# Repacking attention outputs before normalizing them, two blocks at a time

## The chip, the cores and the metric

The kernel runs on one core of a Trainium2 chip. The metric is the time of one execution on the device, in microseconds (us); lower is better. The kernel before was timed three times: 1481.99, 1484.75 and 1485.82 us, median 1484.75. One further execution was profiled.

The core has five engines that run beside each other: PE (TensorE, matrix products), ACT (ScalarE, functions such as the exponential), DVE (VectorE), POOL (GpSimd) and SP (SyncE, which here only issues DMAs). Matrix products are written to PSUM, which has eight banks; everything else lies in SBUF.

## The reference, cut to what matters

Two equal layers, each an attention part A and a part B, with one set of weights for both:

```
x = x + A(layernorm(x))
x = x + B(layernorm(x))
x = x + A(layernorm(x))
x = x + B(layernorm(x))

A: q = (x @ wq) as 32 heads of 16;  k = x @ wk;  v = x @ wv    (one k and v for all heads)
   p = softmax(q k^T * 16**-0.5);  o = p v;  return o @ wo
B: h = gelu(layernorm(x) @ w1); each quarter of h is shifted by 1, -1, 2 or -2 rows; hs = h @ w2
   x1 = x + hs;  return x1 + gelu(layernorm(x1) @ w3) @ w4
```

x has 2048 rows (128-row tiles 0 to 15) of 512 columns in bfloat16. The softmax is over 2048 keys, for 32 heads and 2048 queries. Its denominator can be divided out after the product with v, and that division is what the change is about.

## The kernel before, in words

**Chunks, blocks, halves.** The queries of a layer are worked on in chunks of 512 rows (the last 512 of layer 1 as two chunks of 256). A chunk has eight blocks of four heads. A block goes over 16 key tiles of 128 keys; one key tile (two of them in a 256-row chunk) gives two halves of two heads each. There are 2048 halves in the program.

**Two ways for a half.** As a unit (`declare_unit`): PE makes the scores in two PSUM banks, ACT takes the exponential of 128x1024 scores at once (L1125), PE multiplies it with v (L1230). As a pair (`declare_pair`): PE makes the scores of each head in one of three shared banks, DVE turns each into the bits of an approximate exponential (L1143, two per half), POOL, or DVE when POOL is behind, makes two shifted copies (L1180), and PE multiplies all three with scaled copies of v (L1230). The shares on ACT and on DVE follow from the rules below. A column of ones in v gives the denominator as an extra row.

**The end of a block** (`block_end`). The sums lie in bank ACC: four strips of 32 partitions, of which the first 16 are the outputs of one head for half of the queries and row 16 is the denominator. DVE copies them to ACCF (L1264; blocks that had been put aside between the layers are added from there, L1260). PE gathers the denominators as columns (L1274), DVE takes reciprocals into RZ (L1281), PE spreads each over 32 partitions by a product with the identity (L1289), and DVE multiplies ACCF with that into OS (L1295). Then eight DMAs from SP repack OS into OT (L1318), where the output projection (`outproj`, L676 with L1450) wants 16 rows per head. For the last three blocks of a layer's last chunk (`LATE_OT` = 5) PE repacks with a selection matrix (L1308) and DVE copies the result to OT (L1314). When all eight blocks of a chunk are done, `chunk_end` declares the output projection, part B and, at the end of layer 0, the next layer's normalization, keys and values (`next_kv`: `ln_in`, `kv`, with the keys written at L943). This is called side work.

**Between the layers.** While the side work of layer 0's last chunk runs, layer 1 starts with the keys that are there: seven blocks (`SPILLED`) over key tiles 0 to 5 and then 6 to 10 (`EARLY`), their sums put aside (L1248, L1242) and added later.

**What sets the order.** Before anything is emitted, a planner simulates the engines with a duration for each operation and picks, engine by engine, the ready operation with the lowest priority number. The result is one fixed list of instructions per engine, with semaphore waits. Exponentials and their scores come first, then products with v, then pairs and side work. `assign` decides when a pair is started: `MAX_PAIRS` in flight, a limit on DVE's waiting side work (`BACKLOG`), two free shared banks. These and other rules change every 12.5 us of planned time, by one character of the string `TEMPER`, which picks a row of `MOODS`; characters 7, e and f are rows with three pairs in flight. Between the layers (layer 1, first chunk, key tiles below 11) the pair rule is `CALM`, whatever the row says: at most one pair in flight, backlog at most 1. Where PE would be idle too long the planner inserts filler products (L676, ONES and NIL)[...].[...]

Of the kernel before, what the change touches and what calls it, by code (L numbers as in the profile page):

```python
# [10 lines left out]
ALU = mybir.AluOpType  # L11
# [498 lines left out]
def t_ps(n):  # L510
    return 0.066 + n * 1.043e-3
# [6 lines left out]
def t_x2(n):  # L518
    return 0.066 + n * 0.522e-3
# [6 lines left out]
def tiled(n, k=1):  # L526
    return ("P", n * k, n * k, range(4))
# [6 lines left out]
class Kernel:  # L534
# [19 lines left out]
    CALM = (1, 1)  # L554
    CALM_END = (2, 1)
    LATE_OT = 5
# [33 lines left out]
    TEMPER = "090ee27f7f97f71e3eee4ee77f547c4fe941e77e7385715f85317197105502005897e0e10e0ef77f27f593f70f1f030e1e77ee0975325855000003"  # L590
# [9 lines left out]
    def sb(self, name, shape, dtype=dt.bfloat16):  # L600
        n = 1
        for s in shape:
            n *= s
        ap = self.stack.enter_context(self.nc.sbuf_tensor(name, [128, n], dtype))[:, :]
        self.sbytes += n * dt.size(dtype)
        return self.shaped(ap, shape)
# [9 lines left out]
    def memory(self):  # L616
        self.sbytes = 0
        sb = self.sb
# [19 lines left out]
        self.OS = sb("OS", [1024])  # L638
# [13 lines left out]
        self.RZ = sb("RZ", [32])  # L652
# [14 lines left out]
        p = self.par(1, 1)  # L667
# [42 lines left out]
    def head(self):  # L710
        pl = self.pl
        op = pl.op
        ins = self.ins
# [14 lines left out]
        def fill(eng, ap, v, tags, dur, prio):  # L728
            op(eng, lambda e: e.memset(ap, v), writes=tags, dur=dur, prio=prio)
# [38 lines left out]
        fill("POOL", self.SELC, 0.0, [("SELC",)], 0.1, 3)  # L768
        op("POOL", lambda e: e.affine_select(out=self.SELC, in_=self.SELC, compare_op=ALU.not_equal,
# [249 lines left out]
    def make_groups(self):  # L1019
# [49 lines left out]
        self.fin_left = {}  # L1069
        self.main_done = False  # L1070
# [167 lines left out]
    def block_end(self, la, c, b, end):  # L1238
# [13 lines left out]
        nq = n // 128  # L1252
        m = self.nfin % (1024 // n)
        self.nfin += 1
        parts = range(2 * m, 2 * m + 2) if n == 512 else (m,)
        am, zm, om = ([(x, i) for i in parts] for x in ("ACCF", "RZ", "OS"))
        acc, rz, osm = self.ACCF[:, m * n:m * n + n], self.RZ[:, 4 * nq * m:4 * nq * (m + 1)], self.OS[:, m * n:m * n + n]
# [8 lines left out]
        fin = min(5, self.RUSH[la][c])  # L1266
        L = Late()
# [11 lines left out]
        def frec(e):  # L1279
            with self.nc.allow_low_precision("the reciprocals feed a bf16 matmul"):  # L1280
                return e.reciprocal(rz, self.PB[:, L.bank, 0:4 * nq])  # L1281
        op("DVE", frec, writes=[L] + zm, dur=0.17, prio=fin, give=L)
        M = Late()
        for h in range(nq // 2):
            def fx(e, h=h):
                ins = None
                for q in (2 * h, 2 * h + 1):
                    for g in range(4):
                        ins = e.matmul(self.PB[32 * g:32 * g + 32, M.bank, q * 128:(q + 1) * 128],  # L1289
                                       lhsT=rz[:, 4 * q + g:4 * q + g + 1].to_broadcast([128, 32]),  # L1290
                                       rhs=self.IDENT, start=True, stop=True, tile_position=(0, 32 * g))
                return ins
            op("PE", fx, reads=zm + [("ID",)], writes=[M], pe=("P", 256, 256, range(4)), prio=fin,
               take=M if h == 0 else None)
        op("DVE", lambda e: e.tensor_tensor(out=osm, in0=acc, in1=self.PB[:, M.bank, 0:n],  # L1295
                                            op=ALU.mult),
           reads=am, writes=[M] + om, dur=t_ps(n), prio=fin, give=M)
        r0 = 64 * (b % 2)
        hw = n // 2
        if c == len(self.CHUNKS[la]) - 1 and b >= self.LATE_OT:  # L1300
            N = Late()

            def fo(e):
                ins = None
                for u in range(2):
                    for p in range(2):
                        x = r0 + 32 * p
                        ins = e.matmul(self.PB[x:x + 32, N.bank, u * hw:u * hw + hw], lhsT=self.SELO[:, u, :],  # L1308
                                       rhs=osm[:, p * hw:p * hw + hw], start=True, stop=True,
                                       tile_position=(0, x), skip_group_check=True)  # L1310
                return ins
            op("PE", fo, reads=om + [("SELO", i, u) for i in range(2) for u in range(2)], writes=[N],
               pe=("P", 2 * hw, hw, (r0 // 32, r0 // 32 + 1)), prio=fin, take=N)
            op("DVE", lambda e: e.tensor_copy(self.OT[r0:r0 + 64, b // 2, 0:n], self.PB[r0:r0 + 64, N.bank, 0:n]),  # L1314
               writes=[N, ("OT", b)], dur=t_ps(n), prio=fin, give=N)
        else:
            op("SP", lambda e: [
                e.dma_start(self.OT[r0 + 16 * (2 * p + i):r0 + 16 * (2 * p + i) + 16, b // 2, u * hw:u * hw + hw],  # L1318
                            osm[32 * (2 * i + u):32 * (2 * i + u) + 16, p * hw:p * hw + hw])
                for p in range(2) for i in range(2) for u in range(2)],  # L1320
               reads=om, writes=[("OT", b)], dma=128 * n, parts=8, prio=fin)
# [6 lines left out]
        if not left:  # L1328
            self.chunk_end(la, c)

# [309 lines left out]
```

## Time and profile before

| | |
|---|---|
| median of three runs | 1484.75 us (1481.99 to 1485.82) |
| the profiled execution's own time | 1481.02 us |
| its span in the profile | 1479.2 us |
| PE busy | 1454.1 us |
| ACT busy | 1421.3 us |
| DVE busy | 1285.0 us |
| POOL busy | 1146.2 us |
| exponentials on ACT (L1125) | 1419 |
| evictions of pairs on DVE (L1143) | 1258 |
| TensorE clock granted | 0.999 of full speed |

A line of the groups names the source line, engine and operation, what is written and from what, the shapes (partitions x elements), the count, then the busy time in us and the mean of one in ns, then the idle time of the engine just before them and what ended it. The mean of one can be longer than busy time divided by count, since neighbours overlap. Busy PE is not PE at its peak. In a table of windows a row has the window's start, end and length, then for each engine busy time and count in brackets (PE, weight loads, DVE, ACT, POOL), then the clock, the DMA share and GB/s.

### The profile page before, as it was taken

What the parts mean: (1) busy time and instruction counts of PE and PEld (TensorE: products, weight loads), DVE (VectorE), ACT (ScalarE), POOL (GpSimd) and SP (SyncE); (2) the same over time, 40 slices, a digit from 0 to 9 for tenths busy, and PEclk for the clock granted to TensorE, in tenths of its full rate; (3) what the DMA queues carried; (4) which work ended last, traced back from release to release, by engine and by line L of the source; (5) the groups of instructions that cost most, each with busy time, mean ns of one, the idle gap of its engine ahead of it and who ended that gap; (6) DMA issues with size and microseconds to landing.
All of it is one profiled execution on the core that took longest, in us unless ns stands there. A gap on an engine that the chain in (4) does not pass through costs nothing.

```text
span 1479.2 us, 66152 instructions
## 1 busy us (share of the span) xinstructions
PE 1454.1 (98%) x30189; PEld 651.1 (44%) x30189; DVE 1285.0 (87%) x2304; ACT 1421.3 (96%) x1511; POOL 1146.2 (77%) x817
## 2 busy tenths in 40 slices
PE   9999999999999999999999999999999999999999
PEld 4443434444444444444344444444444445555555
DVE  8989999989999979887886799999889989888863
ACT  7999999999999999999999999999999999999962
POOL 2788888878889878797765588889678898888640
PEclk9999999999999999999999999999999999999999
DMA  6100100001000000100000000010000000000000
GB/s 216 29 6 6 21 6 6 5 6 20 7 4 6 6 4 7 20 5 2 3 2 3 3 8 12 5 21 5 10 18 8 4 6 7 13 19 11 6 14 25
DMA packets 32153, 21.71 MB, mean 15 GB/s; under 512 B 12672, under 2 KB 31360, under 8 KB 31872
## 3 DMA queue, kind: packets, MB, share of 16 engines
q1 hardware_dynamic: 31872, 17.47, 5.0%
q8 instruction: 236, 3.87, 1.1%
q14 instruction: 45, 0.37, 0.1%
HBM read 7.90 MB, written 2.10 MB: 7 GB/s over the span
## 4 chain that ended last, share of the span: by engine, by line
ACT 74%; PE 21%; DVE 3%; POOL 1%; issue 0%; DMA 0%; POOLq 0%
ACT EA L1125 69%; PE PB L676 7%; PE PB L1081 7%; PE PB L1230 6%; ACT G L1573 3%; ACT L1125 1%; DVE J L1143 1%; ACT GP L1493 1%; POOL J L1180 1%; ACT L1573 1%; ACT L1493 1%; PE PB L875 1%; DVE ST L791 0%; DVE G L1568 0%; PE PB L932 0%
## 5 line engine op out<-in xcount | busy, mean ns | idle before, releaser
L1125 ACT ACTIVATE EA<-PB 128x1024 bf16<-128x1024 f32 x1419 | 1305.2, 1169 | 11.3 <-PE PB L1081 5.3
L1180 POOL TENSOR_SCALAR J<-J 128x2048 uint16<-128x2048 uint16 (+1 forms) x556 | 1006.1, 1810 | 233.5 <-DVE J L1143 126.4
L1143 DVE TENSOR_SCALAR J<-PB 128x512 uint16<-128x512 f32 x1258 | 808.5, 682 | 84.3 <-PE PB L1081 79.0
L1081 PE MATMUL PB<-QT,KT 32*128 32x512 bf16 (+1 forms) x4608 | 606.0, 360 | 13.7 <-ACT EA L1125 5.7
L1230 PE MATMUL PB<-J,VD 128*32 128x256 bf16 (+1 forms) x8448 | 413.9, 265 | 2.1 <-POOL J L1180 0.8
L1230 PE MATMUL PB<-EA,VP 128*32 128x256 bf16 (+1 forms) x6400 | 350.8, 263 | 0.7 <-DVE KT L1242 0.4
L1081 PEld LDWEIGHTS PB<-QT,KT 32*128 32x128 bf16 x4608 | 162.7, 91 | 385.0 <-ACT EA L1125 316.6
L1230 PEld LDWEIGHTS PB<-J,VD 128*32 128x32 bf16 x8448 | 176.1, 95 | 176.0 <-issue 133.9
L1230 PEld LDWEIGHTS PB<-EA,VP 128*32 128x32 bf16 x6400 | 150.3, 95 | 114.0 <-issue 90.9
L676 PE MATMUL PB<-ZT,W 128*32 128x512 bf16 (+2 forms) x2816 | 171.1, 342 | 0.2
L676 PE MATMUL PB<-W,G 128*32 128x512 bf16 x1624 | 104.2, 381 | 0.6 <-ACT G L1573 0.6
L1180 DVE TENSOR_SCALAR J<-J 128x2048 uint16<-128x2048 uint16 (+1 forms) x107 | 78.9, 737 | 8.8 <-POOL J L1180 7.9
L1568 DVE CAST G<-PB 128x512 bf16<-128x512 f32 (+2 forms) x126 | 72.5, 582 | 13.5 <-PE PB L676 12.2
L676 PEld LDWEIGHTS PB<-ZT,W 128*32 128x32 bf16 x2816 | 63.6, 96 | 33.5 <-issue 21.3
L811 POOL TENSOR_TENSOR SM<-SM,MH 128x2 f32<-128x2 f32 (+1 forms) x69 | 49.6, 722 | 22.2 <-DVE SM L813 13.5
L1573 ACT ACTIVATE G<-G 128x1792 bf16<-128x1792 bf16 x29 | 47.0, 1685 | 15.4 <-DVE G L1568 15.3
L676 PEld LDWEIGHTS PB<-W,G 128*32 128x32 bf16 x1624 | 37.5, 96 | 39.1 <-issue 11.6
L1295 DVE TENSOR_TENSOR OS<-ACCF,PB 128x512 bf16<-128x512 bf16 (+1 forms) x72 | 44.7, 621 | 7.3 <-PE PB L1289 7.0
L676 PE MATMUL PB<-ONES,NIL 128*32 128x512 bf16 x532 | 49.1, 400 | 1.6 <-DVE J L1143 0.5
L791 DVE BATCH_NORM_STATS2 ST<-X 128x6 f32<-128x512 bf16 x64 | 43.1, 681 | 1.8 <-DMA X<-in_A_x_dram 1.3
L1549 POOL TENSOR_TENSOR X<-Y,X 128x512 bf16<-128x512 bf16 x32 | 38.6, 1218 | 6.3 <-DVE Y L1531 4.6
L1264 DVE CAST ACCF<-PB 128x512 bf16<-128x512 f32 (+1 forms) x65 | 40.0, 615 | 2.5 <-PE PB L1230 2.4
(103 smaller groups left out, 765.7 us busy)
## 6 DMA issues: line engine op xcount, KB each, us to landing
OT<-OS SPq DMA_DIRECT2D x424, 8.0 KB, 1.8
W<-in_B_w_dram SPq DMA_DIRECT2D x2, 1792.0 KB, 14.9
X<-in_A_x_dram SPq DMA_DIRECT2D x8, 256.0 KB, 4.7
QT<-QS SPq DMA_DIRECT2D x32, 64.0 KB, 2.4
out_dram<-OUTB SPq DMA_DIRECT2D x16, 128.0 KB, 1.7
OT<-OS SPq DMA_DIRECT2D x104, 4.0 KB, 2.2
W<-in_B_w_dram SPq DMA_DIRECT2D x2, 512.0 KB, 9.3
WQ<-in_A_wq_dram SPq DMA_DIRECT2D x1, 512.0 KB, 4.1
```

Source lines behind the costliest of these rows:

```text
L676: ins = e.matmul(self.PB[32 * g:32 * g + 32, bank, 0:n], lhsT=lhsT[:, 32 * g:32 * g + 32], rhs=rhs, start=start, stop=stop, tile_position= ...
L791: op("DVE", lambda e, tb=tb: e.bn_stats(self.ST6[:, tb, :], src(tb)), reads=[tagf(tb)], writes=[("ST", tb)], dur=0.606, prio=prio)
L811: op("POOL", lambda e: e.tensor_tensor(out=out, in0=src, in1=self.MH[:, 0, a:b], op=ALU.pow), reads=tags + [("MH",)], writes=tg(r), dur=0. ...
L1081: ins = e.matmul(self.PB[:, bank, j * n:(j + 1) * n], lhsT=self.KT[32 * h:32 * h + 32, la, (kb + j) * 128:(kb + j + 1) * 128], rhs=self.QT ...
L1125: o = q.feeds = op("ACT", lambda e: e.activation(self.EA[:, ea, :, :], self.PB[:, b0:b0 + 2, :], ACTF.Exp, scale=0.25), writes=bk + [("EA" ...
L1143: o = op("DVE", lambda e, i=i, L=L: e.tensor_scalar(out=self.J[:, 3 * s, i * 512:(i + 1) * 512], in0=self.PB[:, L.bank, :], scalar1=128 * ...
L1180: o = self.pl.op(eng, lambda e: e.tensor_scalar(out=self.J[:, d, :], in0=self.J[:, f, :], scalar1=float(self.STEP), scalar2=1.0, op0=ALU.a ...
L1230: ins = e.matmul(self.PB[32 * x:32 * x + 32, self.ACC, p * hw:p * hw + hw], lhsT=v[:, la, kb + j, :], rhs=ap[:, i, j * w + u * hw:j * w + ...
L1264: self.last_copy = op("DVE", lambda e: e.tensor_copy(acc, self.PB[:, self.ACC, 0:n]), writes=[("AC",)] + am, dur=t_ps(n), prio=0, side=False)
L1295: op("DVE", lambda e: e.tensor_tensor(out=osm, in0=acc, in1=self.PB[:, M.bank, 0:n], op=ALU.mult), reads=am, writes=[M] + om, dur=t_ps(n), ...
L1568: op("DVE", lambda e, f=f, L=L: e.tensor_copy(self.G2[:, f, 0:n], self.PB[:, L.bank, 0:n]), writes=[L] + [(x, f, i) for x in ("G2", "GE") ...
L1573: op("ACT", lambda e, i=i: e.activation(self.G2[:, :, i * 128:(i + 1) * 128], self.G2[:, :, i * 128:(i + 1) * 128], ACTF.Gelu_apprx_tanh), ...
```

## The change

The raw outputs are repacked first: for a block that goes by DMA, the eight DMAs now read ACCF, right after it is written. The reciprocals stay in a table RZ with a place for each of the eight blocks, zeroed once at the start. When both blocks of a pair of neighbours have their reciprocals, `scale_pair` copies the two blocks' reciprocals into RZE, each value 16 times (a DVE copy of 512 elements), PE spreads them over the layout that OT has, and DVE multiplies OT in place. So two blocks share one spreading step and one product. The blocks that PE repacks (now the last two of a layer's last chunk, `LATE_OT` = 6) keep their own spreading and product, in place in ACCF (`repack`). The buffer OS is gone. `CALM` allows two pairs in flight, and there is a new `TEMPER` string, with 62 characters of 7, e or f among its 118, where the old one has 52.

```diff
-    CALM = (1, 1)
+    CALM = (2, 1)
-    LATE_OT = 5
+    LATE_OT = 6
-    TEMPER = "090ee27f7f97f71e3eee4ee77f547c4fe941e77e7385715f85317197105502005897e0e10e0ef77f27f593f70f1f030e1e77ee0975325855000003"
+    TEMPER = "12075e7f7ef97777f9e130e77e2038fe10f0fef7fee336fee27ee71e2353e005544f971fef071750377ede7f07f04ee3eee01709ef9ef1f8000000"
...
-        self.OS = sb("OS", [1024])
-        self.RZ = sb("RZ", [32])
+        self.RZ = sb("RZ", [2, 8, 8])
+        self.RZE = sb("RZE", [32, 16])
...
+        fill("POOL", self.RZ, 0.0, [("RZ", b) for b in range(8)], 0.1, 3)
...
+        late = c == len(self.CHUNKS[la]) - 1 and b >= self.LATE_OT
+        if not late:
+            op("SP", lambda e: [
+                e.dma_start(self.OT[r0 + 16 * (2 * p + i):r0 + 16 * (2 * p + i) + 16, b // 2, u * hw:u * hw + hw],
+                            acc[32 * (2 * i + u):32 * (2 * i + u) + 16, p * hw:p * hw + hw])
+                for p in range(2) for i in range(2) for u in range(2)],
+               reads=am, writes=[("OT", b)], dma=128 * n, parts=8, prio=fin)
...
-                return e.reciprocal(rz, self.PB[:, L.bank, 0:4 * nq])
-        op("DVE", frec, writes=[L] + zm, dur=0.17, prio=fin, give=L)
+                return e.reciprocal(self.RZ[:, :, b, 0:2 * nq].rearrange("p i (q u) -> p q i u", u=2),
+                                    self.PB[:, L.bank, 0:4 * nq].rearrange("p (q i u) -> p q i u", i=2, u=2))
+        op("DVE", frec, writes=[L, ("RZ", b)], dur=0.17, prio=fin, give=L)
+        if late:
+            self.repack(b, n, acc, am, fin)
         else:
-            op("SP", lambda e: [
-                e.dma_start(self.OT[r0 + 16 * (2 * p + i):r0 + 16 * (2 * p + i) + 16, b // 2, u * hw:u * hw + hw],
-                            osm[32 * (2 * i + u):32 * (2 * i + u) + 16, p * hw:p * hw + hw])
-                for p in range(2) for i in range(2) for u in range(2)],
-               reads=om, writes=[("OT", b)], dma=128 * n, parts=8, prio=fin)
+            key = (la, c, b // 2)
+            if key in self.half_done:
+                self.scale_pair(b // 2, n, fin)
+            self.half_done.add(key)
...
+    def scale_pair(self, k, n, fin):
...
+            for u in range(2):
+                for s in range(ns):
+                    j = u * ns + s
+                    for g in range(4):
+                        z = 8 * (g // 2) + 2 * ((g % 2) * ns + s) + u
+                        ins = e.matmul(self.PB[32 * g:32 * g + 32, M.bank, j * 128:(j + 1) * 128], lhsT=self.RZE[:, :, z],
+                                       rhs=self.IDENT, start=True, stop=True, tile_position=(0, 32 * g))
...
+        op("DVE", lambda e: e.tensor_copy(
+            self.RZE.rearrange("p (i d) z -> p i d z", i=2),
+            self.RZ[:, :, b0:b0 + 2, :].rearrange("p i b z -> p i (b z)").unsqueeze(2).to_broadcast([128, 2, 16, 16])),
+           reads=[("RZ", b0), ("RZ", b0 + 1)], writes=[("RZE",)], dur=t_x2(512), prio=fin)
+        op("PE", fx, reads=[("RZE",), ("ID",)], writes=[M], pe=tiled(n), prio=fin, take=M)
+        ot = self.OT[:, k, 0:n]
+        op("DVE", lambda e: e.tensor_tensor(out=ot, in0=ot, in1=self.PB[:, M.bank, 0:n], op=ALU.mult),
+           writes=[M, ("OT", b0), ("OT", b0 + 1)], dur=t_ps(n), prio=fin, give=M)
```

`repack` holds what the old code did for a block that PE repacks: the two steps of L1289, the product of L1295 (now written back to ACCF), the selection of L1308 and the copy of L1314.

More of the change, by code (lines that the diff above doesn't have):

```diff
@@ L1069, in make_groups @@
         self.fin_left = {}
+        self.half_done = set()
         self.main_done = False
@@ L1252, in block_end @@
         nq = n // 128
+        hw = n // 2
+        r0 = 64 * (b % 2)
         m = self.nfin % (1024 // n)
@@ L1255, in block_end @@
         parts = range(2 * m, 2 * m + 2) if n == 512 else (m,)
-        am, zm, om = ([(x, i) for i in parts] for x in ("ACCF", "RZ", "OS"))
-        acc, rz, osm = self.ACCF[:, m * n:m * n + n], self.RZ[:, 4 * nq * m:4 * nq * (m + 1)], self.OS[:, m * n:m * n + n]
+        am = [("ACCF", i) for i in parts]
+        acc = self.ACCF[:, m * n:m * n + n]
         if end == "add":
@@ L1280, in frec @@
             with self.nc.allow_low_precision("the reciprocals feed a bf16 matmul"):
-                return e.reciprocal(rz, self.PB[:, L.bank, 0:4 * nq])
-        op("DVE", frec, writes=[L] + zm, dur=0.17, prio=fin, give=L)
[L1283 to L1315, printed above, removed]
-        else:
-            op("SP", lambda e: [
-                e.dma_start(self.OT[r0 + 16 * (2 * p + i):r0 + 16 * (2 * p + i) + 16, b // 2, u * hw:u * hw + hw],
-                            osm[32 * (2 * i + u):32 * (2 * i + u) + 16, p * hw:p * hw + hw])
-                for p in range(2) for i in range(2) for u in range(2)],
-               reads=om, writes=[("OT", b)], dma=128 * n, parts=8, prio=fin)
@@ L1329, in block_end, with fx @@
             self.chunk_end(la, c)
+    def scale_pair(self, k, n, fin):
+        op = self.pl.op
+        M = Late()
+        ns = n // 256
+        b0 = 2 * k
+        def fx(e):
+            ins = None
+            for u in range(2):
[5 more added lines that the diff above has]
+                                       rhs=self.IDENT, start=True, stop=True, tile_position=(0, 32 * g))
+            return ins
+        op("DVE", lambda e: e.tensor_copy(
[6 more added lines that the diff above has]
+           writes=[M, ("OT", b0), ("OT", b0 + 1)], dur=t_ps(n), prio=fin, give=M)
@@ new lines, in repack, with fx, fo @@
+    def repack(self, b, n, acc, am, fin):
+        op = self.pl.op
+        nq = n // 128
+        hw = n // 2
+        r0 = 64 * (b % 2)
+        M = Late()
+        for h in range(nq // 2):
+            def fx(e, h=h):
+                ins = None
+                for q in (2 * h, 2 * h + 1):
+                    for g in range(4):
+                        ins = e.matmul(self.PB[32 * g:32 * g + 32, M.bank, q * 128:(q + 1) * 128],
+                                       lhsT=self.RZ[:, g // 2, b, 2 * q + g % 2:2 * q + g % 2 + 1].to_broadcast([128, 32]),
+                                       rhs=self.IDENT, start=True, stop=True, tile_position=(0, 32 * g))
+                return ins
+            op("PE", fx, reads=[("RZ", b), ("ID",)], writes=[M], pe=("P", 256, 256, range(4)), prio=fin,
+               take=M if h == 0 else None)
+        op("DVE", lambda e: e.tensor_tensor(out=acc, in0=acc, in1=self.PB[:, M.bank, 0:n], op=ALU.mult),
+           writes=[M] + am, dur=t_ps(n), prio=fin, give=M)
+        N = Late()
+        def fo(e):
+            ins = None
+            for u in range(2):
+                for p in range(2):
+                    x = r0 + 32 * p
+                    ins = e.matmul(self.PB[x:x + 32, N.bank, u * hw:u * hw + hw], lhsT=self.SELO[:, u, :],
+                                   rhs=acc[:, p * hw:p * hw + hw], start=True, stop=True,
+                                   tile_position=(0, x), skip_group_check=True)
+            return ins
+        op("PE", fo, reads=am + [("SELO", i, u) for i in range(2) for u in range(2)], writes=[N],
+           pe=("P", 2 * hw, hw, (r0 // 32, r0 // 32 + 1)), prio=fin, take=N)
+        op("DVE", lambda e: e.tensor_copy(self.OT[r0:r0 + 64, b // 2, 0:n], self.PB[r0:r0 + 64, N.bank, 0:n]),
+           writes=[N, ("OT", b)], dur=t_ps(n), prio=fin, give=N)
```

## The prediction

> **What bounds the kernel now.** I read the page's totals and slices first.
>
> ```profile
> span 1479.2 us, 66152 instructions
> PE 1454.1 (98%) x30189; PEld 651.1 (44%) x30189; DVE 1285.0 (87%) x2304; ACT 1421.3 (96%) x1511; POOL 1146.2 (77%) x817
> ...
> DVE  8989999989999979887886799999889989888863
> ACT  7999999999999999999999999999999999999962
> ...
> ACT 74%; PE 21%; DVE 3%; POOL 1%; issue 0%; DMA 0%; POOLq 0%
> ```
>
> ACT and PE are both nearly full, and the chain that ended last runs on ACT for 74% of the span. ACT's digits fall only in the first slice and the last two. So I asked for ACT's pieces in order of time (start, length, then the idle time before it in brackets).
>
> ```profile
> 35.36 186.19 ACT L1125 ACTIVATE EA<-PB 128x1024 bf16<-128x1024 f32 x203 [0.56 <-PE PB L1081]
> ...
> 767.52 23.94 ACT L1125 ACTIVATE EA<-PB 128x1024 bf16<-128x1024 f32 x26 [1.37 <-PE PB L1230]
> 815.25 7.44 ACT L1125 ACTIVATE EA<-PB 128x1024 bf16<-128x1024 f32 x8 [2.44 <-PE PB L1230]
> ...
> 1423.88 6.46 ACT L1573 ACTIVATE G<-G 128x1792 bf16<-128x1792 bf16 x4 [2.01 <-DVE G L1568]
> ```
>
> Between 35.4 and 1420.6 us ACT idles about 7 us in all. One exponential of a half costs 186.19/203 = 0.917 us. The span is therefore a head of 35 us, 1385 us of ACT without a gap, and a tail of 58 us after the last exponential. In the middle only one thing shortens time: fewer halves on ACT, that is more pairs on DVE. The groups by form give the prices.
>
> ```profile
> L1125 ACT ACTIVATE EA<-PB 128x1024 bf16<-128x1024 f32 x1419 | 1305.2, 1169 | 11.3 <-PE PB L1081 5.3 <-PE PB L1230 5.3
> L1143 DVE TENSOR_SCALAR J<-PB 128x512 uint16<-128x512 f32 x1258 | 808.5, 682 | 84.3 <-PE PB L1081 79.0
> L676 PE MATMUL PB<-ONES,NIL 128*32 128x512 bf16 x532 | 49.1, 400 | 1.6 <-DVE J L1143 0.5 <-DVE ZR L828 0.3 <-DVE YT L884 0.2
> L1295 DVE TENSOR_TENSOR OS<-ACCF,PB 128x512 bf16<-128x512 bf16 x56 | 38.1, 680 | 5.2 <-PE PB L1289 4.9
> L1289 PE MATMUL PB<-IDENT,RZ 128*32 128x128 bf16 x1024 | 29.7, 219 | 0.0
> L828 DVE TENSOR_SCALAR Y<-X,MV,SM 128x512 bf16<-128x512 bf16 x32 | 20.4, 650 | 1.0 <-POOL SM L811 1.0
> L1295 DVE TENSOR_TENSOR OS<-ACCF,PB 128x256 bf16<-128x256 bf16 x16 | 6.6, 413 | 2.1 <-PE PB L1289 2.1
> ```
>
> 1419 halves are on ACT and 1258/2 = 629 are pairs, together the 2048 halves of the program. PE's fillers[...] are 49 us, and 25 of these lie before 300 us: PE has some 25 us to spare in the last 1180.
>
> [...]the 128x512 tensor_scalar at L828 has a median of 0.41 us and a worst case of 1.93, and POOL's shifts take 1.90.[...]
>
> **The change part by part.**
>
> *Products.* Before: 72 (56 wide, 16 narrow), 38.1 + 6.6 = 44.7 us of DVE. After, the two last blocks of each layer's last chunk keep their own (2 wide, 2 narrow), and 68 blocks share 34 products (layer 0: 12 + 3 wide; layer 1: 12 wide, 4 + 3 narrow): 29 x 0.680 + 9 x 0.413 = 23.4 us. Saved: 21.3 us. LATE_OT = 6 takes one block per layer off the route over PE: one wide and one narrow cast at L1314 less, 0.69 + 0.42 = 1.1 us.
>
> *Spreading copies.* 34 new DVE copies of 512 bf16 elements. The nearest row is L828's undisturbed 0.41 us: 13.9 us.[...] Net DVE freed: 21.3 + 1.1 - 13.9 = 8.5 us[...].
>
> *The lock.* Where the planner places L828's form and the shifts it marks them[...]; it does not mark the new copy. POOL's shifts are busy 1006 of 1479 us (68%), so a copy placed blindly meets one with that chance and waits 0 to 1.9 us, 0.65 on average over all. The broadcast matmuls wait for it in PE's queue, and the scores of the next half stand behind them; ACT has about half a microsecond in hand, as it works on one half of 0.92 us while the next needs about 0.4. Of a uniform wait the part above 0.3 us (planned margin) + 0.5 us averages 1.1 x 1.1/2/1.9 = 0.32 us, times 0.68, times 34 = 7.4 us at worst; at best nothing[...]. I take 1.0 us: the L828 rows[...] are still only 0.17 us above 0.41 on average, and several copies will fall where no shift runs.
>
> *Broadcasts.* L1289's 1024 matmuls are 128 pieces of eight. The timeline about 1121 us shows the piece after one starting 0.11 us later. After: 27 x 2 + 7 + 2 x 2 + 2 = 67 pieces. 61 x 0.11 = 6.7 us of PE saved, and about 0.2 with the two repacking pieces: 6.9.
>
> *Banks.* Before, a block holds one of the three shared PSUM banks from the broadcast to the product's end: 1121.28 to 1123.06, 1.8 us, 72 times, 130 us. After, a pair's product also waits for the repacking DMA (8 issues of 0.59 us and 1.8 to land, 6.5 us after L1264's cast, to which the planner adds 2.5), while the broadcast can run some 5 us after that cast: 34 holds of about 4 us, 136 us. No gain, no loss; behind that bank stand pairs and side work, and if the planner holds it 2 us longer per pair, 68 us in which pairs start rarely would cost at most some 10 pairs.
>
> *DMAs.* 66 x 8 = 528 become 68 x 8 = 544 issues on SP, and each set starts about 6 us earlier. SP's only others are the query moves and the output; it waits for DVE for over 700 us. Cover: ACCF has two wide slots, next written two blocks (about 40 us) later; OT's old contents are read by the output projection, which ends (207.3 in the first chunk) within 3 us of the next block's cast (204.2), so at most one set of DMAs stands for about that time. In the last chunk block 5 now goes by DMA: cast at 1403.82, rows there by about 1411, product by about 1414, and the output projection cannot start before block 7's at 1424.8. Hidden by 10 us; without that cover it would cost its 9. The memset of RZ and the longer access patterns of the reciprocal: nothing, POOL has 23% and DVE 13% free.
>
> *From freed time to span.* A pair costs DVE 808.5/629 = 1.285 us and 78.9/629 = 0.125 for its shifts: 1.41. So 8.5 us of DVE carry 6.0 more pairs. PE gives the same: a pair instead of an exponential adds two accumulations (0.21 us) and loses about nothing on scores, as its scores run beside another half's: +0.25 (0.1 to 0.43). Equal ends of ACT and PE mean 0.917 n = 6.9 - 0.25 n, n = 5.9. Six pairs: -5.5 us.
>
> *The rule between the layers.* It allowed one pair in flight while layer 1 works on its first 11 key tiles, now two. This stretch, with its rows:
>
> ```profile
> 703.00:816.00 113.00, 111.64 (x2109) 47.25 (x2113) 90.54 (x172) 109.07 (x114) 75.13 (x72) 1.00 0.01 3
> ...
> L1143 DVE TENSOR_SCALAR J<-PB 128x512 uint16<-128x512 f32 x58 | 38.5, 684 | 11.4 <-PE PB L1081 11.1
> L676 PE MATMUL PB<-ONES,NIL 128*32 128x512 bf16 x20 | 1.8, 383 | 0.0
> ```
>
> 29 pairs beside 106 exponentials are 21%, against 31% over the whole kernel. DVE has 20% free there, PE has nothing (111.64 of 113, fillers 1.8). Raised to the average: +12 pairs, -11 us. But PE cannot take them, and the keys of layer 1's last four tiles arrive by the cast at 849.87 (L943), about when ACT needs them. I take 1.5 pairs, -1.4 us; the loss bound is the second rival. The new string gives three pairs in flight to 62 of 118 stretches (52 before); such stretches hold 6.8 pairs now against 5.2 in the others, but DVE and PE set the limit, so I add nothing. The tail: same work, nothing.
>
> *Sum.* -5.5 - 1.4 + 1.0 = -5.9 us. The profiled execution took 1481.02 us, 1.8 more than its span, and would come to 1475.1; it lies 3.7 below the median of 1484.75. On the median: 1478.8.
>
> **Rivals.** The bound for "no change" is 0.3%, 4.5 us, about what a measurement of this kernel can tell.
>
> 1. *Hidden anyway.* The freed PE and DVE time does not become pairs: bank rules allow no more, the fillers grow by the 7 us[...]. For it: 79 us of L1143's waits are for scores, not for a free DVE. Against it: fillers are only some 25 us after 300. Time 1483 to 1486.
>
> 2. *Slower, between the layers.* From 703 to 850 the chain from the last output projection to layer 1's keys goes through some 14 DVE steps in a row (add, statistics, apply, transposed copy, casts, the same for the MLP and the next norm). If each meets one more pair's two evictions, 1.28 us, ahead of it, the keys are 18 us late, and ACT, with fewer exponentials to do before, stands still for it. Net 18 - 5.5: about 1497. It decides once the keys come over 10 us later: 5.5 to undo the gain, 4.5 for the bound. For it: no ACT idle after 827, so the keys are just in time. Against it: side work of that chunk has an urgent priority, and pair evictions already wait for PE there.
>
> 3. *The lock at its worst*: +7.4 in place of 1.0, 1485.2: no change.
>
> **Numbers.** Forecast (more pairs) 0.60, its own range 1470 to 1480.2; hidden or lock 0.17; slower 0.23. Faster 0.60, same 0.17, slower 0.23. The range 1469 to 1492 leaves out about 0.1 at each end: over 16 pairs more, or the keys over 13 us late.
>
> **What would show it.** Right: about 1270 to 1276 evictions at L1143 and 1410 to 1413 exponentials, ACT again without gaps from 35 us, DVE products near 23 us, spreading copies near 0.41, DVE busy about as before. Copies near 1.0 us with PE waiting for them: the lock. An ACT gap near 830 to 860 ended by scores or the key cast: rival 2. The same count of exponentials and more fillers: rival 1. What would make it wrong: a replanned order whose pair count moves by more than these budgets, in either direction.

## The result, and the profile after

The changed kernel takes 1488.15 us (median of 14 runs, 1485.43 to 1495.8) against 1482.88 us for the kernel before in runs beside them (14 runs, 1480.84 to 1485.82). The ratio is 1.004, with a 95% interval from 1.0026 to 1.0053: slower by 0.4%, where 1478.8 us was forecast. The profiled execution took 1486.41 us, with a span of 1484.6 us.

The totals, ACT's row of slices and the chain's first line, from the page of the kernel after:

```profile
span 1484.6 us, 65462 instructions
PE 1451.8 (98%) x29837; PEld 645.4 (43%) x29837; DVE 1312.3 (88%) x2348; ACT 1409.3 (95%) x1494; POOL 1153.6 (78%) x819
...
ACT  7999999999999999999898999999999999999962
...
ACT 45%; PE 38%; DVE 9%; POOL 6%; issue 1%; DMA 0%; POOLq 0%
```

ACT is busy 12 us less than before, and yet the span is 5.4 us longer: ACT stands still more. Its digits now fall below 9 twice in the middle too, and the chain, which ran over ACT for 74% of the span, leaves it for PE, DVE and POOL. The groups by form say how much work moved (busy time and mean of one, then the idle time before them).

```profile
L1127 ACT ACTIVATE EA<-PB 128x1024 bf16<-128x1024 f32 x1402 | 1293.2, 1139 | 27.4 <-PE PB L1083 17.1 <-PE PB L1232 9.4
...
L1145 DVE TENSOR_SCALAR J<-PB 128x512 uint16<-128x512 f32 x1292 | 828.5, 681 | 80.3 <-PE PB L1083 74.5
...
L1328 DVE COPY RZE<-RZ 128x512 bf16<-128x512 bf16 x34 | 26.9, 792 | 0.5
...
L1334 DVE TENSOR_TENSOR OT<-OT,PB 128x512 bf16<-128x512 bf16 x27 | 18.3, 676 | 0.3 <-PE PB L1325 0.2
...
L1325 PE MATMUL PB<-IDENT,RZE 128*32 128x128 bf16 x488 | 13.7, 227 | 0.0
```

There are 1402 exponentials instead of 1419 and 646 pairs instead of 629: 17 more pairs, where 7.5 were forecast. The idle time before exponentials grew from 11.3 to 27.4 us, nearly all of it for PE. And the spreading copies take 0.79 us each, twice my 0.41. ACT in order of time (start, length, idle time before) shows where it stops; five of its gaps:

```profile
663.49 41.53 ACT L1127 ACTIVATE EA<-PB 128x1024 bf16<-128x1024 f32 x45 [1.11 <-PE PB L1083]
...
730.04 1.94 ACT L1127 ACTIVATE EA<-PB 128x1024 bf16<-128x1024 f32 x2 [4.84 <-PE PB L1232]
...
811.18 5.62 ACT L1127 ACTIVATE EA<-PB 128x1024 bf16<-128x1024 f32 x6 [3.10 <-PE PB L1232]
...
1007.56 1.02 ACT L1127 ACTIVATE EA<-PB 128x1024 bf16<-128x1024 f32 x1 [1.40 <-PE PB L1083]
1009.73 2.11 ACT L1127 ACTIVATE EA<-PB 128x1024 bf16<-128x1024 f32 x2 [1.14 <-PE PB L1083]
```

These are three different things: a stop after a copy (663), stops between the layers (730, 811), and a stop with the clock down (1007 to 1010).

**The account.** The closest starts of successive exponentials lie 0.904 us apart. What successive exponentials with no gelu between them lie further apart than that, summed from 36 to 1430 us, I call ACT's *standing still*; it is worked out from the trace. Before: 24.4 us; after: 43.1. Of the 17 exponentials fewer, 16 lie in this stretch and give -14.5 us; standing still gives +18.8. The stretch begins 0.6 us later (at 35.95 in place of 35.36), the passages with gelus take 0.3 more in all, and the tail from the start of the last exponential is 59.9 us against 59.7. Sum +5.4, which is the difference of the spans. The pairs came, and more was lost in waits than they gave.

**The mechanism of one copy.** The timeline of the kernel after about 660 us, all engines, left out where nothing bears on it:

```profile
659.50 7.87 POOL L1182 TENSOR_SCALAR J<-J 128x2048 uint16<-128x2048 uint16 x4 [1.18 <-DVE J L1182]
659.61 1.93 DVE L1328 COPY RZE<-RZ 128x512 bf16<-128x512 bf16 x1
...
661.46 0.67 DVE L1610 CAST G<-PB 128x512 bf16<-128x512 f32 x1
662.06 5.48 DVE L1145 TENSOR_SCALAR J<-PB 128x512 uint16<-128x512 f32 x9
...
662.19 0.38 PE L1083 MATMUL PB<-QT,KT 32*128 32x512 bf16 x1 [1.07 <-DVE G L1610]
...
663.49 4.86 ACT L1127 ACTIVATE EA<-PB 128x1024 bf16<-128x1024 f32 x5 [1.11 <-PE PB L1083]
```

POOL's shift starts 0.11 us ahead of the copy, and the copy lasts 1.93 us, about a shift's 1.90. Behind it on DVE stands the cast of G, which frees a PSUM bank; the next scores on PE (662.19) need that bank; the scores of the next exponential stand behind them in PE's fixed order and come 0.9 us later. Copy 1.93, PE idle 1.07, ACT idle 1.11.

Of the 34 copies 13 take 0.28 to 0.35 us, 5 take up to 0.74, and 16 take 0.82 to 1.93. When each of these 16 began, a shift was running on POOL, and each ended 0.14 to 0.15 us after that shift: it is the shift that they wait for. This wait is what the prediction and what follows call the lock; what in the chip makes it, no trace shows. The 16 waited 15.4 us beyond 0.29. After 14 of them ACT stands still within 6 us, about 10.7 us in all (stops of over 0.1 us counted).

### The profile page after: what moved, and what is told of

Same layout as the page of the kernel before. It is cut to its first block, busy times and chain, and to the rows that moved or that the text cites. A ratio compares the mean times of both kernels' runs of the same rounds, so it can differ in the third digit from the quotient of the medians.

```text
span 1484.6 us, 65462 instructions
## 1 busy us (share of the span) xinstructions
PE 1451.8 (98%) x29837; PEld 645.4 (43%) x29837; DVE 1312.3 (88%) x2348; ACT 1409.3 (95%) x1494; POOL 1153.6 (78%) x819
## 4 chain that ended last, share of the span: by engine, by line
ACT 45%; PE 38%; DVE 9%; POOL 6%; issue 1%; DMA 0%; POOLq 0%
ACT EA L1127 41%; PE PB L1083 13%; PE PB L1232 12%; PE PB L676 11%; DVE J L1145 5%; POOL J L1182 4%; ACT G L1615 2%; DVE RZE L1328 1%; POOL SM L812 1%; ACT L1127 1%; PE PB L876 1%; DVE G L1610 1%; DVE J L1182 0%; PE PB L1009 0%; ACT GP L1535 0%
## 5 line engine op out<-in xcount | busy, mean ns | idle before, releaser
L1127 ACT ACTIVATE EA<-PB 128x1024 bf16<-128x1024 f32 x1402 | 1293.2, 1139 | 27.4 <-PE PB L1083 17.1
L1182 POOL TENSOR_SCALAR J<-J 128x2048 uint16<-128x2048 uint16 (+1 forms) x557 | 1014.1, 1821 | 227.0 <-DVE J L1145 95.2
L1145 DVE TENSOR_SCALAR J<-PB 128x512 uint16<-128x512 f32 x1292 | 828.5, 681 | 80.3 <-PE PB L1083 74.5
L1083 PE MATMUL PB<-QT,KT 32*128 32x512 bf16 (+1 forms) x4608 | 605.5, 360 | 15.6 <-ACT EA L1127 5.0
L1232 PE MATMUL PB<-J,VD 128*32 128x256 bf16 (+1 forms) x8688 | 421.2, 265 | 3.7 <-POOL J L1182 1.9
L1182 DVE TENSOR_SCALAR J<-J 128x2048 uint16<-128x2048 uint16 (+1 forms) x119 | 83.5, 702 | 7.1 <-POOL J L1182 6.3
L1610 DVE CAST G<-PB 128x512 bf16<-128x512 f32 (+2 forms) x126 | 72.0, 580 | 10.2 <-PE PB L676 9.2
L676 PE MATMUL PB<-ONES,NIL 128*32 128x512 bf16 x516 | 46.1, 400 | 0.6 <-DVE ZR L829 0.3
L1268 DVE CAST ACCF<-PB 128x512 bf16<-128x512 f32 (+1 forms) x65 | 39.9, 615 | 2.2 <-PE PB L1232 2.2
L1641 DVE TENSOR_TENSOR OUTB<-PB,X 128x512 bf16<-128x512 f32 x16 | 11.0, 685 | 32.3 <-PE PB L676 32.3
```

Of the source, the lines that this page charges most:

```text
L676: ins = e.matmul(self.PB[32 * g:32 * g + 32, bank, 0:n], lhsT=lhsT[:, 32 * g:32 * g + 32], rhs=rhs, start=start, stop=stop, tile_position= ...
L1083: ins = e.matmul(self.PB[:, bank, j * n:(j + 1) * n], lhsT=self.KT[32 * h:32 * h + 32, la, (kb + j) * 128:(kb + j + 1) * 128], rhs=self.QT ...
L1127: o = q.feeds = op("ACT", lambda e: e.activation(self.EA[:, ea, :, :], self.PB[:, b0:b0 + 2, :], ACTF.Exp, scale=0.25), writes=bk + [("EA" ...
L1145: o = op("DVE", lambda e, i=i, L=L: e.tensor_scalar(out=self.J[:, 3 * s, i * 512:(i + 1) * 512], in0=self.PB[:, L.bank, :], scalar1=128 * ...
L1182: o = self.pl.op(eng, lambda e: e.tensor_scalar(out=self.J[:, d, :], in0=self.J[:, f, :], scalar1=float(self.STEP), scalar2=1.0, op0=ALU.a ...
L1232: ins = e.matmul(self.PB[32 * x:32 * x + 32, self.ACC, p * hw:p * hw + hw], lhsT=v[:, la, kb + j, :], rhs=ap[:, i, j * w + u * hw:j * w + ...
```

## The experiments

The question is what of the loss is the lock, and what hides behind the sum. My theory after the result: the copies wait for POOL's shifts, and this costs nearly 10 us, not 1. The rivals: the spread costs by its own work on DVE; the loss lies between the layers; or the freed time never became time saved. Since any change of a planned duration or rule moves the whole plan, and the string of the planner is picked for one plan, all experiments but one (e8) keep the order of every engine as it is.

The table holds the profiled executions: pairs up to the end of layer 1's first chunk (the start of its last cast at L1264 or L1268) and after it, standing still in the same two parts, and the clock lost, which is (1 - granted clock) x 2 us summed over those stretches of 2 us between 36 and 1472 us that show under 0.97.

| kernel | ratio to before | end of that chunk, us | pairs | standing still, us | clock lost, us |
|---|---|---|---|---|---|
| before | 1 | 905.9 | 392.5 + 236.5 | 17.4 + 6.9 | 1.7 |
| after | 1.004 | 904.1 | 407 + 239 | 25.7 + 17.4 | 3.4 |
| e5: spread without a lock | 0.997 | 900.8 | 407 + 239 | 22.0 + 13.0 | 1.7 |
| e6: e5, shifts wait longer | 0.9953 | 900.9 | 407 + 239 | 22.2 + 10.2 | 0 |
| e9: after, shifts wait longer | 1.0011 | 907.2 | 407 + 239 | 28.9 + 14.3 | 1.7 |
| e7: before, shifts wait longer | 1.0019 | 908.7 | 392.5 + 236.5 | 19.9 + 9.8 | 3.4 |
| e8: old rule between the layers | 1.0115 | 912.2 | 395 + 230 | 24.5 + 14.4 | 1.7 |

### e1: the spread taken out

```diff
-        op("DVE", lambda e: e.tensor_copy(
-            self.RZE.rearrange("p (i d) z -> p i d z", i=2),
...
+        op("DVE", lambda e: e.memset(self.RZE[:, 0:8, :], 1.0),
```

> The changed kernel in its own order, with the spreading copy into RZE replaced by a DVE fill of 256 elements of RZE, so the reciprocals are not spread and the outputs are not divided by the denominators[...]. Lock theory: the changed kernel lost about 10.7 us of ACT behind the 14 copies that took 0.8 us or more, so the time falls by 8 to 11 us, to about 1473 to 1476 if the kernel before gives 1483 (ratio to before 0.993 to 0.996). Rival, the stalls come with the new order of instructions (pairs between the layers, PE full): it falls by under 2 us, ratio above 1.002. Rival, the slower weight loads of RZE (143 ns against 97): also under 2 us, since those loads stay.

Measured: 1478.78 us (1475.45 to 1481.08), ratio to before 0.9967, interval 0.9955 to 0.9979, a little short of the 0.993 to 0.996 expected. The fill covers 128 elements, not the 256 of the expectation, and takes 0.165 us every time: it never waits for POOL. The time is 9.4 us below that of the kernel after, for 34 x (0.79 - 0.165) = 21.3 us less on DVE, so the copies cost that much. But this kernel leaves the division by the denominators out, and two things left at once, the lock and the copying itself.

### e2 and e5: the same values, without the lock

A maximum over an axis of length one copies. That such a reduction would not wait for POOL was my guess when e2 was set up; no trace had shown it. e2 does it on 512 bf16 values, e5 on pairs of them read as 256 fp32 values.

```diff
-        op("DVE", lambda e: e.tensor_copy(
...
+        op("DVE", lambda e: e.tensor_reduce(
+            out=self.RZE.rearrange("p d z -> p (d z)").bitcast(dt.float32).rearrange("p (i d z) -> p i d z", i=2, d=16),
+            in_=self.RZ.rearrange("p i b z -> p (i b z)").bitcast(dt.float32).rearrange("p (i b z) -> p i (b z)", i=2, b=8)[
+                :, :, 4 * b0:4 * b0 + 8].unsqueeze(2).unsqueeze(4).to_broadcast([128, 2, 16, 8, 1]),
+            op=ALU.max, axis=mybir.AxisListType.X),
```

> The changed kernel in its own order, with the spreading done by a DVE maximum over an axis of one element, which reads and writes the same values[...]. Lock theory: no copy above 0.7 us,[...] ACT loses at most 3 us for it, so 6 to 10 us below the changed kernel, ratio to before 0.993 to 0.998. If only DVE's total time counted[...]: ratio 1.002 to 1.004.

> The kernel after in its own order; only the spreading copy (L1328) is replaced by a max over an axis of length one on pairs of bf16 values read as one fp32 number, 256 elements instead of 512, the same values written. Lock theory (the copies wait for POOL's shifts, and ACT stands still behind them): the spreading takes 0.33 to 0.42 us each with no long ones, and the time comes to 1478 to 1481 us, ratio to before 0.996 to 0.998; against the slow reduction of 512 elements (1482.26) some 2 to 4 us less, because 34 x 0.3 us of DVE are saved. If the gain of the memset run came from the missing spread rather than from the missing lock: 1485 to 1488.

Measured: e2 1482.26 us (14 runs), ratio 0.9991 (0.9982 to 1.0); e5 1478.53 us (22 runs), ratio 0.997 (0.9962 to 0.9979). The group of the spread in e5, and the same place in the order as in the timeline above, on DVE:

```profile
L1328 DVE TENSOR_REDUCE RZE<-RZ 128x256 f32<-128x256 f32 x34 | 14.0, 413 | 0.5
```

```profile
657.62 0.42 DVE L1328 TENSOR_REDUCE RZE<-RZ 128x256 f32<-128x256 f32 x1
657.96 0.68 DVE L1612 CAST G<-PB 128x512 bf16<-128x512 f32 x1
```

(L1612 is the cast at L1610 of the kernel after.) All 34 take between 0.40 and 0.42 us; not one waits. The cast of G follows 0.34 us after the spread begins, not 1.85, and ACT's stop of 1.11 us is gone. Behind the 16 spreads that were the long copies of the kernel after, ACT stands still for 1.3 us in all, in place of 10.7. A spread that takes longer undisturbed than the copy (0.41 against 0.28 at best) makes the kernel 9.6 us faster than the kernel after by the medians. The prediction's 13.9 us of DVE for the spread is just what e5 spends (14.0), so e5 is the changed kernel as the prediction had priced it, less the 1.0 us for the lock. That the copying itself is the cost is refuted; the lock is shown. e2 (0.68 us each), which spends 9 us more of DVE than e5, is slower than it by 3.7 us, and still 5.9 us faster than the kernel after, just under the 6 to 10 expected.

### e3 and e4: copies in the kernel before

The reverse: the kernel before in its order, with 18 copies of 512 elements behind reciprocals (16 in layer 0, 2 in layer 1's first chunk), written to a buffer that nobody reads until the end. e4 has fills of 256 elements there.

```diff
-                return e.reciprocal(rz, self.PB[:, L.bank, 0:4 * nq])
+                ins = e.reciprocal(rz, self.PB[:, L.bank, 0:4 * nq])
+                if la == 0 and b in (1, 3, 5, 7) or la == 1 and c == 0 and b in (3, 5):
+                    ins = e.tensor_copy(self.OUTB[:, 0, :], self.ONES)
+                return ins
```

> The kernel before in its own order, with one more DVE copy of 512 bf16 elements between SBUF tensors (constants, to a buffer that is free then) right behind the reciprocal of 18 blocks: four of each chunk of layer 0 and two of layer 1's first chunk. The planner knows nothing of it. Lock theory: the copies meet POOL's shifts with a chance of two thirds, wait up to 1.6 us, and ACT loses 0.3 to 0.4 us for each on average: 4 to 8 us slower (ratio 1.003 to 1.006). If an unplanned 0.3 us on DVE is harmless and no lock stands behind the loss: under 1.5 us, the same as the fill of the next run.

> The same as the run before, with a DVE fill of 256 elements in place of the copy: the same unplanned time on DVE (about 0.3 us)[...]. Lock theory: under 1.5 us slower than the kernel before (ratio below 1.001), and 3 to 7 us faster than the copy. Rival (unplanned DVE work of any kind costs): as slow as the copy.

Measured: e3 1501.92 us, ratio 1.0124 (1.0111 to 1.0137), +19 us; e4 1484.36, ratio 1.0012 (1.0004 to 1.002), +1.5. The fills take 0.27 us. The copies' group in e3, and two stretches of it from the copy at 112.0 us (PE, PEld, DVE, ACT and POOL busy, then the granted clock):

```profile
L1283 DVE COPY OUTB<-ONES 128x512 bf16<-128x512 bf16 x18 | 18.3, 1019 | 0.0
```

```profile
112.00:116.00 4.00, 2.62 (x65) 1.25 (x57) 3.54 (x5) 2.67 (x4) 3.10 (x2) 0.97 0.02 4
116.00:120.00 4.00, 4.00 (x56) 1.39 (x53) 3.40 (x7) 3.23 (x4) 2.37 (x2) 0.60 0.06 11
```

The copies wait as in the kernel after, 1.02 us on average, and cost 1.06 us of time each: my 4 to 8 us were far too few. The stretches say why. The copy of 1.80 us at 112.0 holds PE for 1.38 us (2.62 of 4 us busy), and then, when PE is full again, the clock is at half for some 3.4 us. That happens after four of the 18 copies, and at two places more where no copy is near (230 and 408 us); the clock lost is 10.2 us in e3 against 1.7 before. Such a copy can be paid twice, once as a wait and once as a slow stretch that follows it. That copies placed blindly cost this much is shown; since these copies stand ahead of a block's broadcasts and not ahead of a pair's, the price per copy isn't that of the kernel after.

### e6, e9, e10 and e7: races lost to POOL's shifts

The stop at 1004 to 1010 us in the kernel after has no copy in it. DVE's, POOL's and PE's timelines there, and then two stretches of 3.4 us:

```profile
1004.00 2.09 DVE L829 TENSOR_SCALAR ZR<-Y,MV,SM 128x512 bf16<-128x512 bf16 x1
...
1004.05 1.90 POOL L1182 TENSOR_SCALAR J<-J 128x2048 uint16<-128x2048 uint16 x1
...
1006.15 0.62 PE L876 MATMUL PB<-IDENT,ZR 128*32 128x128 bf16 x16 [1.37 <-DVE ZR L829]
```

```profile
1003.40:1006.80 3.40, 2.01 (x46) 0.93 (x42) 3.33 (x4) 2.77 (x4) 2.46 (x2) 0.89 0.02 5
1006.80:1010.20 3.40, 3.40 (x34) 0.73 (x30) 2.18 (x4) 1.49 (x2) 2.68 (x2) 0.50 0.00 0
```

The planner marks some operations of DVE and POOL, the shifts and the normalization at L829 among them (`port=True`), and moves those of the two engines apart. L829 has 0.41 us undisturbed. Here it takes 2.09, though it starts, as recorded, 0.05 us before the shift: DVE lost the race, and why, the trace does not show. PE stands for 1.37 us, the clock falls to half, and ACT loses some 4 us. The planner has a rule for this: a shift planned just behind such an operation of DVE waits for the DVE operation *before* it. I let it wait for the operation itself, in e5 (e6), in the kernel after (e9), in e1 (e10) and in the kernel before (e7); the order stays, only these waits differ.

```diff
-                o.preds.add(self.order["DVE"][-2])
+                o.preds.add(self.order["DVE"][-1])
```

> As the run before it in this list, and one rule of the planner is changed: a POOL shift planned to start just after a DVE operation[...] waits for that operation itself, not for the one before it on DVE. The order of every engine is the same, only these waits differ. Theory that lost races[...] (L829 taking 2.1 us at about 1004 and 1343 us, after which the granted clock is 0.5 to 0.6 for some 7 us) cost the kernel after 3 to 6 us: no L829 above 1.9 us, no stretch under 0.7 of the clock, 3 to 6 us less than the run before it (1473 to 1477). Rival, that these races cost nothing because POOL's waits come back elsewhere: within 1 us of it.

> The kernel after with its locking spreading copies; only the planner's wait rule for POOL's shifts is changed (a shift planned to start just after a DVE operation[...] waits for that operation). Order as in the kernel after. Theory, that the lost race at 1004 us costs about 3.8 us and the rule mends it: 1483 to 1485.5, ratio to before 1.000 to 1.002, L829 under 1.95 us near 1004. Rival, that a gain of this rule is luck of where idle PE time falls for the granted clock (in the kernel before the rule lost 2.8 us): anything from 1484 to 1490, and the stretches at half clock move to other places instead of going.

> The memset run (e1: the spread is replaced by filling a quarter of RZE with ones, so the reciprocals are not spread and the outputs not divided) with the changed wait rule. e1 was at 1478.78 and had two lost races (1000 and 1346 us) with 5.1 us of clock lost. If the rule mends lost races: 1473 to 1475.5 and no stretch at half clock there. If its gain in e6 was luck of the clock: 1477 to 1480.

> The kernel before in its own order with the same change of the planner's wait rule for POOL's shifts. The kernel before shows one such lost race (L828 at 395.5 us, 1.14 us, clock 0.71 to 0.82 beside it) and a worst L828 of 1.93 us. Theory: 1 to 3 us less than before (ratio 0.998 to 0.9995). Rival, the rule costs POOL as much as it saves DVE: ratio 0.9995 to 1.001. If it gains as much as in the kernel after, the rule has nothing to do with the change and is not the reason for its loss.

Measured: e6 1476.02 us (5 runs), ratio 0.9953 (0.9941 to 0.9965), 2.5 us less than e5. e9 ratio 1.0011 (1.0002 to 1.0019) in place of 1.004: 0.0029, or 4.3 us. e10 1476.31 us, ratio 0.9948 (0.9935 to 0.996) in place of e1's 0.9967: 2.8 us. e7 1486.04 us, ratio 1.0019 (1.0011 to 1.0026): 2.8 us *more*. In e6 the same two operations, on DVE and POOL:

```profile
999.30 0.41 DVE L829 TENSOR_SCALAR ZR<-Y,MV,SM 128x512 bf16<-128x512 bf16 x1
...
999.80 3.88 POOL L1182 TENSOR_SCALAR J<-J 128x2048 uint16<-128x2048 uint16 x2 [0.54 <-DVE ZR L829]
```

This race is mended and POOL pays 0.54 us for it. Others are not (L829 still takes 2.04 us at 555 us in e6, where I expected none above 1.9; the race at 1343 us that the expectation gives to the kernel after is one of e1 and e5), and the gains of e6 and e10 are under the 3 us and more that I expected. The profiles of e6 and e10 show no stretch at half clock at all, and e6 beats both kernels. The intervals of e9 and after don't overlap; those of e6 and e5, and of e10 and e1, overlap a little. What the rule gains is the clock: the five runs of e5 with a mean clock of 1.000 have a median of 1476.1 us, the five of e6, all at 1.000, one of 1476.0, while the two runs of e5 at 0.995 took 1483.1. And e7 forbids to call the rule a gain as such. The same two stretches, first of the kernel before, then of e7:

```profile
218.00:222.00 4.00, 3.28 (x38) 1.00 (x34) 3.88 (x7) 3.54 (x4) 3.67 (x5) 1.00 0.01 2
...
226.00:230.00 4.00, 3.78 (x92) 2.00 (x90) 3.95 (x8) 4.00 (x5) 3.74 (x4) 1.00 0.02 6
```

```profile
218.00:222.00 4.00, 3.20 (x42) 1.05 (x38) 3.81 (x8) 3.82 (x5) 3.64 (x5) 1.00 0.01 2
...
226.00:230.00 4.00, 4.00 (x74) 1.84 (x72) 2.18 (x4) 3.07 (x3) 3.74 (x4) 0.50 0.02 4
```

The work is the same and 0.3 us later; PE idles as much just before 222 us (0.21 and then 0.45 us, in both kernels). In one the clock stays at 1.00, in the other it halves, and standing still between 200 and 300 us is 4.7 us against 2.2. That is about half of what e7's profiled execution stands still longer (29.7 against 24.4 us); 2.9 us more lie in layer 1 without a slow clock, and no run names their cause. The same stop is followed by half clock in e3 (0.50 from 232 to 234 us) and e4 (0.50 from 224 to 226) too. But in e4 the stretch at half clock that the kernel before has at 395 us is gone in return, and the clock lost is 1.7 us in both: e4's 1.5 us are not explained by it. In e9, too, a stretch at half clock (3.4 us from 665.5) appears after the copy of 660 us that the kernel after doesn't have there, and the one at 1006 is gone.

How long PE stood does not tell these cases apart. The stretches at half clock between 36 and 1472 us, in all twelve profiles, last some 3.4 or 6.8 us (394.65 to 398.06 us in the kernel before, 1006.06 to 1012.89 in the kernel after); in e3 they begin at 74.80, 115.76 and 153.30 us, 12 and 11 times 3.413 apart. For the kernels before and after I cut the time between 36 and 1472 us into steps of 3.413 us, laid so that these stretches fill whole steps, and added up the columns that PE's matmuls stream in each (512 for a 128x512; one that crosses a border counts by its share). The median step has some 20,700.

| step from, us | its clock | columns | PE busy | clock of the next step |
|---|---|---|---|---|
| after, 1002.6 | full | 11,410 | 0.62 | half |
| after, 1006.1 | half | 9,870 | 0.97 | half |
| after, 1009.5 | half | 12,480 | 1.00 | full |
| before, 391.2 | full | 10,710 | 0.75 | half |
| before, 394.7 | half | 12,880 | 1.00 | full |
| after, 661.3 (behind the copy) | full | 12,770 | 0.74 | full |
| before, 217.2 | full | 13,650 | 0.92 | full |
| before, 220.6 (the stop at 221) | full | 14,190 | 0.84 | full |

The steps of 661.3 and 217.2 have the fewest columns of all those at full clock, after and before, that were followed by full clock. PE's busy share doesn't sort the steps: 0.75 was followed by half clock, 0.74 was not. In e7 the 3.413 us that hold the stop at 221 us, up to the drop of the clock, have about 11,800 columns, counted from its timeline, where the kernel before has 14,190; e7 stands still 2.5 us longer there. The same work, 0.3 us later, was followed by another clock. The count was made after the runs, on few drops, and none of the runs varied it on purpose: what sets the clock is not shown.

### e8: the old rule between the layers

```diff
-    CALM = (2, 1)
+    CALM = (1, 1)
```

> The kernel after with the old rule between the layers (one pair in flight during layer 1's first key tiles) put back; since a changed rule moves everything planned behind it, the string of the planner was picked again from that stretch on, less thoroughly than that of the kernel after, so that only the stretch from layer 0's last chunk to the end of layer 1's first compares: 375.0 us in the kernel after, 385.2 in the kernel before. If dropping the rule gives that gain (10 pairs more for 5 us more of ACT's standing still): 380 to 386 us here, and ACT's gaps in it near 5 us. If the gain of that stretch comes from the cheaper products alone: 374 to 377 us, with gaps near 10. The whole is expected slower than the kernel after, 1490 to 1505, because of the string.

Measured: 1499.95 us, ratio 1.0115 (1.0102 to 1.0129). The stretch from layer 0's last chunk to the end of layer 1's first takes 382.5 us instead of 375.0, within the 380 to 386 of the theory. Two of ACT's gaps there:

```profile
762.27 13.86 ACT L1127 ACTIVATE EA<-PB 128x1024 bf16<-128x1024 f32 x15 [1.11 <-PE PB L1232]
...
801.58 6.52 ACT L1127 ACTIVATE EA<-PB 128x1024 bf16<-128x1024 f32 x7 [2.64 <-PE PB L1232]
```

The stop of 4.84 us at 730 isn't here. Standing still within layer 1's first chunk is 8.2 us in e8, 12.1 after and 6.7 before; the 5 us that I expected were too few. Against 12 fewer pairs (395 instead of 407 by the end of the chunk) this leaves the rule's end worth about 7.5 us there. The string was picked again from there on, and one of its characters differs within the stretch (at 762.5 us of planned time), so the size is less sure than the sign, and the total says nothing. One correction to my own expectation: the 385.2 us of the kernel before are no measure of that stretch, because a batch of gelu that ACT runs at 522 us before lies at 512 after, ahead of the stretch's begin. The chunk's end, 905.9 before and 904.1 after, has both in it.

## Why the prediction was wrong

**The step that failed is the lock: "I take 1.0 us".** It cost 9.6 us by the medians of after and e5; by the ratios 0.0070 x 1483 = 10.4, and between e9 and e6, which have the mended races, 0.0058 x 1483 = 8.6. Among runs with a mean clock of 1.000 e9 (seven, median 1485.3 us) and e6 (five, 1476.0) differ by 9.3: the waits alone cost about 9 us. Without the lock the prediction's sign is right: e5 stands at 1478.5 us, 4.4 us under the kernel before by its ratio. By the prediction's own terms:

- *How long a copy waits*: "0.65 on average over all". Measured (0.79 - 0.29) = 0.50. Right enough; the copies were placed blindly, and 28 of the 34 began while a shift ran, where POOL's 68% said 23.
- *What ACT has in hand*: "0.3 us (planned margin) + 0.5 us". Here the size fell. Waits of 15.4 us in 16 copies turned into 10.7 us of standing still; 16 x 0.3 is all that was in hand. ACT's half microsecond, which I had added to it, was not there; it may be that a full DVE queue has it used up already, but no run shows this.
- *Who waits*: "The broadcast matmuls wait for it in PE's queue". The trace shows no such wait: PE's idle time before the 488 matmuls at L1325 is 0.0 us. What waits is DVE's own queue: casts and evictions that free PSUM banks, and through these the scores. So the cost hangs on what stands behind the copy on DVE.
- *The choice*: 1.0 out of 0 to 7.4, because the L828 rows showed little waiting. But the planner keeps these apart from the shifts, and the copies not; the row was a wrong likeness, and the prediction itself says that the copy is not marked. Even the upper end was too low, because it took off the half microsecond: with the 0.3 us alone the same formula gives 0.68 x 34 x 1.6 x 1.6/2/1.9 = 15.6 us. And it knew nothing of the clock that can fall after a PE stop, as in e3 (0.60 from 116 to 120 us).

**That the total without the lock hit 1478.5 is partly luck.** Without its 1.0 us for the lock the prediction had -6.9 us, and e5 gained 4.4; the base was 1484.75, the median of three runs, which is 1.9 above that of 14. And other terms were off, in both directions:

- *The rule between the layers*: "I take 1.5 pairs, -1.4 us". It let in about 12 pairs and is worth about 7.5 us net (e8). The reason given, that PE cannot take them, was half right: PE took them, and ACT waited for it. In the stretch shown in the prediction PE is as full as before and the evictions did not grow. The stretch, of the kernel after:

```profile
703.00:816.00 113.00, 111.43 (x2259) 52.74 (x2251) 94.87 (x190) 101.86 (x103) 68.47 (x68) 1.00 0.01 3
```

In it are 57 evictions at L1145 against 58, and ACT is busy 7 us less: other work of PE is done in this stretch, and the stops at 730 and 811 wait for PE. Against the kernel before, the additional pairs come after it (layer 1's first chunk has 76 against 66). Against e8, which has the old rule in the new plan, most of them lie in it: e8 has 39 evictions there, 9 pairs fewer, with PE as full (112.05 of 113 us).

- *Freed DVE and PE*: "Six pairs: -5.5 us". After the first chunk of layer 1 there are only 2.5 more pairs, worth -2.3 us, and in e5 standing still grows there by 6.1: from 905.9 us to the end before takes 573.3 us, e5 from 900.8 takes 576.2. e6 gets 2.8 of this back. For the rest, about 3 us of small stops, no run names a cause; it stays open. "Hidden anyway" was thus in part true for layer 1, though not with its sign, more fillers: they are 46.1 us in the kernel after against 49.1.
- *Banks*: "34 holds of about 4 us, 136 us. No gain, no loss". From the first matmul at L1325 to the end of the product at L1334 the 34 holds take 83 us in all, against 116 for the 72 before. What this is worth no run shows.

**What held.** The products: 23.4 us forecast, 23.3 measured (the row of L1334 above, with 7 narrow ones and the four of the last blocks). The tail: 59.9 against 59.7 us, so the repacking DMAs are hidden in the last chunk. An undisturbed spread took 0.28 us at best, under the 0.41 that it was priced at. DVE is busy 27 us more, not about as before: 34 more evictions are 20 us of it, its own shifts at L1182 take 4.6 more (83.5 against 78.9), and the copies with their waits use up (26.9) what the products and casts give.

**The rivals.** The third, the lock at its worst, named the cause; its 1485.2 us were 3 too few. The second ended on the right side for the wrong reason: no gap lies between 830 and 860, and the cast for layer 1's last keys comes at 841.0 us, earlier than before (849.9). The stops between the layers are those at 730 and 811, when PE has other work.

## What to carry to other kernels

When an operation is added to a kernel with a full POOL, look first in a trace whether its form waits for POOL (here the copy took up to 1.93 us and the tensor_scalar of L829 up to 2.09, e5's maximum never more than 0.42 and e1's fill always 0.165), and price its wait by what stands behind it on DVE's queue, not by when its result is needed; a form that is slower undisturbed and never waits (0.41 us in place of 0.28) was worth 9.6 us here. Take the waits of operations that a planner keeps apart from POOL's as no sign for those that it does not. And look at the granted clock of each run, and after each stop of PE, before a small difference is put down to the change: a stretch at half clock was worth 2 to 4 us, as much as the effects that one wants to tell apart, and comparing runs with the same mean clock took it out.

## What the runs showed of the hardware that I had not expected

- After PE stops of 0.4 to 1.4 us the granted clock was at 0.50 for 3.4 or 6.8 us, with PE full (1.38 us at 112 in e3, 1.37 at 1005 in the kernel after). The same stop of 0.45 us at 221 us left the clock at 1.00 in the kernel before and was followed by 0.50 in e7.
- The runs of one kernel differ mostly by this: the kernel after took 1485.4 us at a mean clock of 0.999 and 1495.8 at 0.991.
- All 16 long copies ended 0.14 to 0.15 us after the shift that was running when they began.
- An operation on DVE that by its recorded start was 0.05 us ahead of POOL's shift waited for all of it (2.09 us in place of 0.41).
- The broadcast's weight loads, whose columns lie 16 elements apart in RZE, take 144 ns each, against 97 for the compact ones of the kernel before; PE had no idle time before the products that use them.
